# 512-query passes, row-tiled scores in a six-bank ring, and a convolution with half the weight loads

## The chip, the cores and the metric

The kernel runs on one core of one Trainium2 chip. The metric is the device time of one execution in microseconds (us). A ratio is always taken between kernels that ran on one chip in the same rounds. Engines are named as in the profile: PE is the matrix engine, PEld its weight loads, DVE VectorE, ACT ScalarE, POOL GpSimd, and SP the engine that issues most DMAs. "L594" is line 594 of that kernel.

## The reference

Two independent halves share the program. Half A is a long convolution, half B is attention with 32 heads of only 20 channels. Cut to what matters:

```python
S, D = 2048, 640                       # B = 1, bfloat16
def A(q, k, v, shift_k, ssm_k, ssm_D):
    kv = causal_fir4(k, shift_k) * v                   # 4 taps per channel
    y  = causal_conv(kv, ssm_k)                        # 2048 taps per channel (by FFT in the reference)
    return q * (y + kv * ssm_D)
def B(x, wqkv, wo):                                    # H = 32 heads, Dh = 20
    q, k, v = heads(x @ wqkv)
    p = softmax(q @ k.T * Dh**-0.5)                    # 32 x 2048 x 2048 exponentials
    return concat(p @ v) @ wo
out = concatenate([A, B], axis=-1)
```

The exponentials alone are 32 x 2048 x 2048 elements. On 128 partitions that is 1024 activations of 128x1024.

## The kernel before

Attention works in 1024 steps over (256 queries, group of four heads, 128 keys). A step computes scores for four heads at once with a block-diagonal Q (`QBD`), so that the 128-row array multiplies mostly zeros. It takes one exponential of 128x1024 and, every third step, the values of three steps. The convolution runs as filler between steps: it is a Toeplitz matrix product per quad of four channels, 64 matmuls with 64 weight loads, whose weights are overlapping windows of the taps. These "tap loads" read the same taps 32 times, each time shifted by one element.

```python
def hk_load(qi, waits=()):                       # tap loads of one channel quad
    for X, ch in enumerate(quad_channels(qi)):   # four channels, one DMA each
        src_ = _ap(kext_ap, [[1, 32], [1, HKW]], offset=ch * KXL)
        dst = HKring[32 * X:32 * X + 32, slot, :]
        ... sp.dma_start(dst, src_)
...
def S_group(n):                                  # scores of a step: two matmuls, 128 x 512
    lhsT = KT_all[:, g, kb * 128:(kb + 1) * 128]
    for qb in range(2):
        ins = pe.matmul(o, lhsT, QBD[:, g % 2, qb, :], start=True, stop=True)
...
# loop: EXP(n); S_group(n + 2); every third step PV_group x 3; then fillers with a budget of 620 ns
for dl in range(NTB):                            # 16 x 4 convolution matmuls per quad
    for q in range(4):
        lhsT = HKring[:, slot, col0:col0 + 128]
        ... pe.matmul(bank, lhsT, rhs, ...)      # 64 columns each
```

The softmax here doesn't subtract the row's maximum and nothing guards it: scores larger than these inputs give would overflow.

## Time and profile before

| | us |
|---|---|
| time, median of 3 runs | 1298.89 (1294.61 to 1301.39) |
| profiled span | 1304.2 |
| ACT busy, all exponentials | 1013 |
| PE busy | 1117 |
| first exponential starts | 80.7 |

From the page of the kernel before: busy time by engine, the granted PE clock and the DMA rate in 40 slices of 32.6 us, the chain of waits that ended last, and the groups of the exponentials and of the two largest PE jobs (line, operation, shapes, count; busy us and mean ns of one; idle before it and what ended that idle).

```profile
PE 1117.0 (86%) x17563; PEld 650.2 (50%) x17852; DVE 516.0 (40%) x1138; ACT 1014.5 (78%) x1025; POOL 23.6 (2%) x22
...
PEclk9998999799999998998999999999998998999997
...
GB/s 192 93 110 76 101 102 110 1 79 104 109 115 86 96 111 79 104 110 72 106 104 118 72 94 116 108 91 109 106 116 84 95 105 78 116 53 53 85 36 11
...
PE 68%; DVE 13%; ACT 12%; DMA 3%; issue 3%; SPq 1%; ACTq 0%; DVEq 0%
...
L635 ACT ACTIVATE P_sb<-PS 128x1024 bf16<-128x1024 f32 x1024 | 1013.2, 1024 | 273.3 <-PE PS L618 178.2
L618 PE MATMUL PS<-QBD,KT_all 128*128 128x512 bf16 x1759 | 559.1, 388 | 50.2 <-ACT P_sb L635 30.6
...
L556 PE MATMUL PS<-R,HKring 128*128 128x64 bf16 x10240 | 419.8, 193 | 0.0
```

PE and ACT are both nearly full (86% and 78%), and the chain lies mostly on PE. ACT has the work that cannot shrink. The timeline of the kernel before has one undisturbed run of exponentials near its end:

```profile
1224.46 64.11 ACT L635 ACTIVATE P_sb<-PS 128x1024 bf16<-128x1024 f32 x67
```

64.11 us for 67 exponentials is 0.957 us each, while one alone lasts 1.024 us: they overlap. By this figure ACT could do all 1024 in an estimated 980 us if it were never kept waiting. By stages (columns: stretch, its length, busy us and instructions per engine, granted PE clock, mean busy share of the 16 DMA engines, GB/s):

```profile
core 0: us, PE busy (x) PEld busy (x) DVE busy (x) ACT busy (x) POOL busy (x), PEclk, DMA share, GB/s
600.00:800.00 200.00, 186.89 (x3407) 117.30 (x3463) 70.21 (x152) 170.66 (x173) 0.00 (x0) 0.98 0.37 103
```

173 exponentials in 200 us, instead of the 209 that 0.957 us would allow.

### The profile page before, as it was taken

What the parts mean: (1) busy time and instruction counts of PE and PEld (TensorE: products, weight loads), DVE (VectorE), ACT (ScalarE), POOL (GpSimd) and SP (SyncE); (2) the same over time, 40 slices, a digit from 0 to 9 for tenths busy, and PEclk for the clock granted to TensorE, in tenths of its full rate; (3) what the DMA queues carried; (4) which work ended last, traced back from release to release, by engine and by line L of the source; (5) the groups of instructions that cost most, each with busy time, mean ns of one, the idle gap of its engine ahead of it and who ended that gap; (6) DMA issues with size and microseconds to landing.
All of it is one profiled execution on the core that took longest, in us unless ns stands there. A gap on an engine that the chain in (4) does not pass through costs nothing.

```text
span 1304.2 us, 38928 instructions
## 1 busy us (share of the span) xinstructions
PE 1117.0 (86%) x17563; PEld 650.2 (50%) x17852; DVE 516.0 (40%) x1138; ACT 1014.5 (78%) x1025; POOL 23.6 (2%) x22
## 2 busy tenths in 40 slices
PE   0487777699998998998999889999998998998776
PEld 0254432156665655655656456666665555663222
DVE  0376774533424423433442432443343343224521
ACT  0035568689997897986989779989997886989995
POOL 5100000000000000000000000000000000000000
PEclk9998999799999998998999999999998998999997
DMA  9632334023343342332334234333342332411210
GB/s 192 93 110 76 101 102 110 1 79 104 109 115 86 96 111 79 104 110 72 106 104 118 72 94 116 108 91 109 106 116 84 95 105 78 116 53 53 85 36 11
DMA packets 62260, 120.87 MB, mean 93 GB/s; under 512 B 23009, under 2 KB 40175, under 8 KB 62095
## 3 DMA queue, kind: packets, MB, share of 16 engines
q1 hardware_dynamic: 60974, 114.89, 32.5%
q0 software_dynamic: 1120, 3.48, 1.1%
q8 instruction: 140, 2.29, 0.7%
q14 instruction: 26, 0.20, 0.0%
HBM read 110.26 MB, written 8.03 MB: 91 GB/s over the span
## 4 chain that ended last, share of the span: by engine, by line
PE 68%; DVE 13%; ACT 12%; DMA 3%; issue 3%; SPq 1%; ACTq 0%; DVEq 0%
PE PS L618 25%; PE PS L556 23%; ACT P_sb L635 12%; PE PS L661 9%; PE PS L296 4%; DVE R L525 4%; DVE QBD L341 3%; PE PS L347 3%; DMA Dbc<-in_A_ssm_D_dram 2%; PE PS L769 2%; DVE R L418 2%; DVE R L416 2%; PE PS L682 1%; SPq L229 1%; DVE KT_all L329 1%
## 5 line engine op out<-in xcount | busy, mean ns | idle before, releaser
L635 ACT ACTIVATE P_sb<-PS 128x1024 bf16<-128x1024 f32 x1024 | 1013.2, 1024 | 273.3 <-PE PS L618 178.2
L618 PE MATMUL PS<-QBD,KT_all 128*128 128x512 bf16 x1759 | 559.1, 388 | 50.2 <-ACT P_sb L635 30.6
L556 PEld LDWEIGHTS PS<-R,HKring 128*128 128x128 bf16 x10240 | 373.7, 98 | 141.1 <-issue 50.7
L556 PE MATMUL PS<-R,HKring 128*128 128x64 bf16 x10240 | 419.8, 193 | 0.0
L570 DVE CAST R<-PS 128x64 bf16<-128x64 f32 x160 | 70.5, 440 | 353.3 <-PE PS L556 351.8
L618 PEld LDWEIGHTS PS<-QBD,KT_all 128*128 128x128 bf16 x2048 | 139.0, 98 | 102.4 <-ACT P_sb L635 92.3
L661 PE MATMUL PS<-P_sb,V_sb 128*21 128x256 bf16 x4096 | 184.5, 280 | 2.2 <-ACT P_sb L635 0.6
L661 PEld LDWEIGHTS PS<-P_sb,V_sb 128*21 128x21 bf16 x4096 | 75.4, 91 | 171.5 <-issue 137.8
L341 DVE CAST QBD<-PS 20x256 bf16<-20x256 f32 x256 | 107.6, 420 | 85.8 <-PE PS L347 79.6
L296 PE MATMUL PS<-xT,R 128*128 128x256 bf16 (+1 forms) x300 | 51.4, 310 | 73.0 <-DVE R L264 49.2
L525 DVE CAST R<-PS 32x512 bf16<-32x512 f32 x80 | 103.3, 1291 | 15.6 <-PE PS L514 13.7
L296 PEld LDWEIGHTS PS<-xT,R 128*128 128x128 bf16 x300 | 29.3, 106 | 97.0 <-DVE R L264 49.2
L674 DVE CAST OT_sb<-PS 128x256 bf16<-128x256 f32 x64 | 27.4, 428 | 126.9 <-PE PS L661 126.7
L347 PE MATMUL PS<-xT,Wq_pad 128*128 128x256 bf16 x315 | 47.2, 283 | 30.2 <-DVE R L525 30.2
L347 PEld LDWEIGHTS PS<-xT,Wq_pad 128*128 128x128 bf16 x315 | 30.8, 100 | 48.9 <-DVE R L525 34.2
L774 DVE CAST Bout<-PS 128x320 bf16<-128x320 f32 x32 | 15.7, 492 | 55.7 <-PE PS L769 41.4
L329 DVE CAST KT_all<-PS 128x256 bf16<-128x256 f32 (+1 forms) x60 | 25.4, 439 | 29.3 <-PE PS L296 29.0
L699 DVE RECIPROCAL rden<-PS 128x4 f32<-128x4 bf16 x128 | 23.4, 182 | 28.3 <-PE PS L682 26.1
L682 PE MATMUL PS<-ident,OT_sb 128*128 128x128 bf16 x128 | 19.0, 233 | 17.0 <-DVE QBD L341 10.9
L769 PE MATMUL PS<-Wo_sb,OnT_sb 128*128 128x320 bf16 x160 | 29.8, 321 | 3.6 <-DVE Bout L774 3.0
L706 DVE TENSOR_TENSOR O_norm<-PS,rden 128x80 bf16<-128x80 bf16 x128 | 30.9, 241 | 4.4
L682 PEld LDWEIGHTS PS<-ident,OT_sb 128*128 128x128 bf16 x128 | 8.3, 100 | 47.0 <-DVE QBD L341 38.7
(43 smaller groups left out, 225.1 us busy)
## 6 DMA issues: line engine op xcount, KB each, us to landing
HKring<-kext_scratch SPq DMA_DIRECT2D x640, 134.0 KB, 2.8
R<-in_A_k_dram SPq DMA_DIRECT2D x61, 160.0 KB, 2.6
R<-in_A_v_dram SPq DMA_DIRECT2D x16, 160.0 KB, 3.0
kext_scratch<-in_A_ssm_k_dram POOLq DMA_DIRECT2D x1, 2560.0 KB, 13.4
out_dram<-Bout SPq DMA_DIRECT2D x16, 160.0 KB, 1.8
qstage<-in_A_q_dram SPq DMA_DIRECT2D x16, 160.0 KB, 2.3
out_dram<-Aout SPq DMA_DIRECT2D x16, 160.0 KB, 1.8
R<-in_B_wqkv_dram SPq DMA_DIRECT2D x1, 2400.0 KB, 10.9
```

The costliest lines, as they stand in the source:

```text
L296: ins = pe.matmul(region[:, 0:ncols], lhsT, rhs, start=(idx == 0), stop=(idx == n - 1))
L329: return dv.tensor_copy(KT_all[:, g, c0:c0 + w], region[:, 0:w])
L341: return dv.tensor_copy(dst, srcap)
L347: ev = misc_group_multi(lambda pe: [pe.matmul(misc_ps[:, 0:256], l, r, start=(i == 0), stop=(i == NCC - 1)) for i, (l, r, _) in enumerate( ...
L525: return dv.tensor_copy(dst, src_)
L556: ins = pe.matmul(bank, lhsT, rhs, start=is_first, stop=is_last)
L570: ev = ev_op("dve", dve_p, lambda dv: dv.tensor_copy(dst, src_), [Wt(SEM_CONV, val)])
L618: ins = pe.matmul(o, lhsT, rhs, start=True, stop=True)
L635: ins = act.activation(P_sb[:, pb, :], S_ps[:, par * 1024:(par + 1) * 1024], ACT.Exp, scale=scale)
L661: ins = pe.matmul(o, lhsT, rhs, start=(kb == 0), stop=(kb == NKB - 1), tile_position=(0, 32 * i))
L682: ins = pe.transpose(misc_bf[:, qt * 128:(qt + 1) * 128], OT_sb[:, qt * 128:(qt + 1) * 128], ident[:, :])
L769: ins = pe.matmul(misc_ps[:, 0:320], OnT_sb[:, cc, qt * 128:(qt + 1) * 128], Wo_sb[:, cc, eh * 320:(eh + 1) * 320], start=(cc == 0), stop= ...
```

## The change

Its intent is to relieve PE, so that ACT alone sets the pace. 512-query passes give 512 steps of two exponentials each. Scores become four 20-row matmuls at four row positions of the array. Their results go round a ring of six PSUM banks. All Q and K are projected once, into two full tensors, and x is transposed on PE rather than by DMA. The convolution is rearranged to half the matmuls. The diff rewrites nearly all of the 1000 lines. Its core, with cuts marked:

```diff
-            def fn(pe):
-                ins = None
-                lhsT = KT_all[:, g, kb * 128:(kb + 1) * 128]
-                for qb in range(2):
-                    rhs = QBD[:, g % 2, qb, :]
-                    o = S_ps[:, (2 * par + qb) * 512:(2 * par + qb + 1) * 512]
-                    ins = pe.matmul(o, lhsT, rhs, start=True, stop=True)
+            def pe(e):
+                for u in range(4):
+                    bk = 2 * ((2 * b + u // 2) % 3) + u % 2
+                    ins = e.matmul(bank[bk], KT[32 * u:32 * u + DH, g, kb * 128:(kb + 1) * 128],
+                                   QT[32 * u:32 * u + DH, g, qc * 512:(qc + 1) * 512],
+                                   start=True, stop=True, tile_position=(32 * u, 0))
+                return ins
 ... cut ...
-            for X, ch in enumerate(quad_channels(qi)):
-                src_ = _ap(kext_ap, [[1, 32], [1, HKW]], offset=ch * KXL)
-                dst = HKring[32 * X:32 * X + 32, slot, :]
-                val = ev_op("sp", hk_p[slot], lambda sp, dst=dst, src_=src_: sp.dma_start(dst, src_),
-                            list(waits) if X == 0 else ())
+            P.dma("sp", HK[qd % NHK], ap(kext, [[80 * KXL, 4], [1, 32], [1, HKW]], (320 * B + m) * KXL + 1),
+                  d_hk[qd % NHK], reads=[b_kext], writes=[cv["HK"][qd % NHK]])
 ... cut ...
+                    for d in range(16):
+                        for r1 in range(2):
+                            n = (16 - d) * 4
+                            lhsT = HK[slot][:, 64 + 128 * d - 64 * r1:64 + 128 * d - 64 * r1 + 128]
+                            rhs = sub(KVX[i], [[64, 2], [1, n]], ql * 256 + r1 * 128)
+                            o = sub(bank[MISC], [[256, 2], [1, n]], u * 64 + d * 4)
 ... cut ...
+            if b >= 24 and b % 5 == 0 and kv_next[0] < NKB:
+                kv_task(kv_next[0])
```

The lines inside the loop over d and r1 are cut too. In the loop over steps, all projections that are not needed at once run as fillers through one bank (`MISC`), one or two per step, in the first 93 steps. The convolution follows from step 124 on.

## The prediction

> **What bounds the kernel now.** Profiled span 1304 us. ACT is busy 1014 us (78%), PE 1117 us (86%) (page, part 1). ACT's work is 1024 exponentials of 128x1024, 1.024 us each by the groups; but the timeline shows a run of 67 of them in 64.11 us (from 1224 us), so 0.957 us apart when none waits: a floor of 980 us. The rest is
> - a prologue: the first exponential starts at 80.7 us; the chain of waits shows 13 us of transposing-DMA issues, 31 us until the last input lands, then 20 us of V projection;
> - 80 to 200 us: 71 exponentials only (windows), as K projections and kv fill PE and DVE;
> - 200 to 1200 us: about 0.86 exponentials per us instead of 1.045, losing some 170 us. The chain is 68% PE; ACT idles 273 us, 178 us of it for scores (groups). PE per step: two 512-column score matmuls (0.22 us apart), values, and 17 convolution matmuls 28 to 29 ns apart;
> - 16 us of tail.
>
> **What the change does.** Same 1024 exponentials, in 512 steps of two.
> - Scores: block-diagonal 128-row matmuls become four 20-row, row-tiled matmuls in four banks. If concurrent, 0.25 to 0.3 us per step against 0.86 for the same output. The before trace shows concurrency only for column tiles (12 value matmuls of 256 columns take 0.32 us, a quarter of their serial time). [...]
> - Convolution: 10240 matmuls of 64 columns (about 297 us at 29 ns) become 5120 averaging 68 columns, estimated 188 us, plus 160 small combining matmuls and three DVE operations per four channel quads. The taps loaded stay 86 MB, now within some 300 steps: about 150 GB/s.
> - Cost: three array modes per step instead of two per three. [...] about 0.11 us from the last value matmul to the next convolution one. So 0.35 us per 1.91 us step.
> - A step with convolution: scores 0.27 + values 0.25 + convolution 1.03 + switches 0.35 = 1.9 us, level with ACT's 1.914 us.
> - No transposing DMA; scores start after a quarter of x and a narrow slice of W. But V, K, Q and x transposes, about 122 tasks through one PSUM bank, fall into the first 93 steps.
>
> **Sum (estimates from the durations above).** First exponential at 20 us; floor 980; first 93 steps lose 50 (two tasks per step wait for each other's evacuation; each of 16 kv blocks holds DVE 3.9 us and the bank with it); convolution steps lose 20; tail 15. Total 1085 us.
>
> Predicted **1085 us, range 1050 to 1140** (8 in 10). Chances: faster by over 2% 0.97, within 2% 0.02, slower 0.01.
>
> **What will show it.** Groups: ACT still 1024 x 1.02 us, its idle down from 273 to about 100 us. Chain: ACT above half. Timeline: four score matmuls starting within 0.1 us. First exponential at 15 to 28 us. Windows: 40 to 180 us below 0.9 exponentials per us; the last 150 us at 1.04. Convolution done by about four fifths of the steps, so no tail of it. DMA in the middle 140 to 190 GB/s.
>
> **What would make it wrong.** Row tiles that serialise: scores 0.9 us, 2.3 us per step or more, about 1200 us or above. Switches dearer than 0.11 us, or small-column convolution matmuls slower than 29 ns: each 0.1 us per step adds 20 to 25 us. Tap loads too slow for a five-slot ring. In the other direction, early tasks hidden better than thought: 1045 us.

No term of the sum goes with them: 20 + 980 + 50 + 20 + 15 = 1085 us. The 0.25 to 0.3 us for the scores were the estimate for the case that row tiles run together. The 0.35 us for switches are about three times the 0.11 us seen in the trace; that a further switch costs as much was not shown. The 188 us for the convolution were an estimate too; one from the kernel before (29 ns for 64 columns, taken for fewer columns as well, and 0.22 us per 512 columns above that) comes to about 184 us.

## More of the kernel before

Where medians of different rounds are set side by side, the kernel before, which ran in all of them, had medians of 1294 to 1302 us. The record marks every run used here as fast.

## The result, and the profile after

The changed kernel took 1479.84 us, median of 4 runs (1475.57 to 1481.97), against 1296.75 us for the kernel before on the same chip. The ratio is 1.141 (95% interval 1.137 to 1.146). Ratios are the mean time of one kernel's fast runs over that of the other's of the same rounds, so not quite the ratio of the medians. It is 14% slower, where 16% faster was forecast.

The page of the changed kernel, the same lines as before:

```profile
PE 1015.2 (69%) x11344; PEld 478.6 (32%) x11344; DVE 273.5 (18%) x570; ACT 970.8 (66%) x1027; POOL 123.9 (8%) x100
...
PEclk7569888885685666676666676566666767555555
...
GB/s 143 159 1 37 88 68 91 94 72 109 72 76 106 106 107 106 106 106 106 116 103 109 104 128 109 107 106 106 106 106 106 106 106 94 83 17 1 1 0 19
...
DMA 45%; PE 23%; ACT 19%; DVE 8%; SPq 3%; issue 1%; ACTq 0%; DVEq 0%
DMA R<-kext_scratch 42%; ACT P_sb L430 19%; PE PS L314 6%; PE PS L594 5%; PE PS L418 4%; PE PS L443 4%; SPq L144 3%; PE PS L514 2%; PE PS L333 2%; DVE R L364 1%; DVE R L362 1%; DVE KT L321 1%; DMA R<-kv_scratch 1%; DVE QT L321 1%; DMA R<-in_B_x_dram 1%
...
L430 ACT ACTIVATE P_sb<-PS 128x1024 bf16<-128x1024 f32 x1024 | 968.3, 1056 | 483.8 <-PE PS L418 474.3
L594 PE MATMUL PS<-R 128*128 128x128 bf16 (+15 forms) x5120 | 297.5, 221 | 215.3 <-DMA R<-kext_scratch 215.3
...
L418 PE MATMUL PS<-QT,KT 20*128 20x512 bf16 x2048 | 273.6, 524 | 109.2 <-ACT P_sb L430 104.6
```

PE has less to do, as intended: 1015 us of busy time, at a clock of 0.67 on average against 0.97. The convolution matmuls fell from 10240 to 5120. But ACT now idles 484 us before its exponentials instead of 273. The chain has moved to a DMA, the load from `kext_scratch`, which is the tap load. PE stands still 215 us in front of convolution matmuls for it. The GB/s row of slices has 106 in slice after slice. A rate that constant suggests a ceiling somewhere, and at a share of the DMA engines of only about 0.3:

```profile
600.00:800.00 200.00, 131.68 (x1701) 80.59 (x1699) 16.39 (x37) 111.05 (x116) 21.42 (x16) 0.66 0.31 107
```

One quad of channels in the middle, from the timeline (start, length, engine, line, operation, count, and idle before it; lines of weight loads and DMA issues left out):

```profile
702.36 1.45 PE L594 MATMUL PS<-R 128*128 128x128 bf16 x15 [2.12 <-DMA R<-kext_scratch]
703.74 0.61 PE L418 MATMUL PS<-QT,KT 20*128 20x512 bf16 x4
704.29 0.61 PE L443 MATMUL PS<-P_sb,V_sb 128*21 128x512 bf16 x4
704.41 1.94 ACT L430 ACTIVATE P_sb<-PS 128x1024 bf16<-128x1024 f32 x2 [2.89 <-PE PS L418]
704.83 0.78 PE L594 MATMUL PS<-R 128*128 128x72 bf16 x17
707.50 1.19 PE L594 MATMUL PS<-R 128*128 128x128 bf16 x11 [1.89 <-DMA R<-kext_scratch]
708.62 0.61 PE L418 MATMUL PS<-QT,KT 20*128 20x512 bf16 x4
```

A quad's 32 convolution matmuls begin at 702.36, the next quad's at 707.50 (17 + 15 matmuls between), 5.1 us later. PE waits 1.89 us for the load. ACT waits 2.89 us, because the next scores stand in PE's queue behind the waiting convolution. The four score matmuls, at a granted clock of 0.50 here (702 to 710 us), run together: 0.61 us for four. A convolution off the critical path has become the critical path, because the scores are issued behind it on PE and start only after it (708.62 after 707.50).

The load moves 4 x 32 rows of 4224 bytes, 540,672 bytes. At 106 GB/s that takes 5.1 us, the period seen. The trace's packet records show packets of 4224 bytes with a median duration of 164 ns; from 600 to 800 us exactly four of them are in flight for 87% of the time. 4224 bytes in 164 ns is 25.8 GB/s; four of them make 103 GB/s. The first dimension of the load, `[80 * KXL, 4]`, is four as well. That it decides over how many DMA engines a load is spread was the assumption at this point, not yet shown. The kernel before has 32 in that place; its packet records show 16 tap packets in flight at once for 13% of the time from 600 to 800 us, and none for 49%.

### The profile page after: what moved, and what is told of

Same layout as the page of the kernel before. It is cut to its first block, busy times and chain, and to the rows that moved or that the text cites. A ratio compares the mean times of both kernels' runs of the same rounds, so it can differ in the third digit from the quotient of the medians.

```text
span 1480.1 us, 24848 instructions
## 1 busy us (share of the span) xinstructions
PE 1015.2 (69%) x11344; PEld 478.6 (32%) x11344; DVE 273.5 (18%) x570; ACT 970.8 (66%) x1027; POOL 123.9 (8%) x100
## 4 chain that ended last, share of the span: by engine, by line
DMA 45%; PE 23%; ACT 19%; DVE 8%; SPq 3%; issue 1%; ACTq 0%; DVEq 0%
DMA R<-kext_scratch 42%; ACT P_sb L430 19%; PE PS L314 6%; PE PS L594 5%; PE PS L418 4%; PE PS L443 4%; SPq L144 3%; PE PS L514 2%; PE PS L333 2%; DVE R L364 1%; DVE R L362 1%; DVE KT L321 1%; DMA R<-kv_scratch 1%; DVE QT L321 1%; DMA R<-in_B_x_dram 1%
## 5 line engine op out<-in xcount | busy, mean ns | idle before, releaser
L430 ACT ACTIVATE P_sb<-PS 128x1024 bf16<-128x1024 f32 x1024 | 968.3, 1056 | 483.8 <-PE PS L418 474.3
L594 PE MATMUL PS<-R 128*128 128x128 bf16 (+15 forms) x5120 | 297.5, 221 | 215.3 <-DMA R<-kext_scratch 215.3
L594 PEld LDWEIGHTS PS<-R 128*128 128x128 bf16 x5120 | 262.9, 115 | 292.0 <-DMA R<-kext_scratch 223.6
L418 PE MATMUL PS<-QT,KT 20*128 20x512 bf16 x2048 | 273.6, 524 | 109.2 <-ACT P_sb L430 104.6
L443 PE MATMUL PS<-P_sb,V_sb 128*21 128x512 bf16 x2048 | 271.2, 521 | 3.7 <-DVE V_sb L338 2.5
L571 POOL COPY R<-R 32x512 bf16<-32x512 bf16 x80 | 107.2, 1339 | 724.8 <-PE PS L594 714.1
L418 PEld LDWEIGHTS PS<-QT,KT 20*128 20x128 bf16 x2048 | 54.4, 96 | 255.9 <-ACT P_sb L430 203.1
L314 PE MATMUL PS<-R 128*20 128x512 bf16 x1280 | 106.3, 475 | 44.0 <-DVE KT L321 10.9
L514 PE MATMUL PS<-Wo_sb,OnT 128*128 128x320 bf16 x160 | 39.0, 401 | 22.9 <-DVE OnT L503 18.3
L333 PE MATMUL PS<-R 128*128 128x240 bf16 (+1 forms) x240 | 35.8, 291 | 16.4 <-DVE V_sb L338 9.2
L333 PEld LDWEIGHTS PS<-R 128*128 128x128 bf16 x240 | 21.3, 109 | 31.8 <-DVE V_sb L338 13.5
```

The costliest lines, as they stand in the source:

```text
L314: ins = e.matmul(bank[bk][32 * i:32 * i + DH, :], W_sb[:, cc, off + i * DH:off + (i + 1) * DH], xT[:, cc, c * 512:(c + 1) * 512], start=(c ...
L333: ins = e.matmul(bank[bk][:, 0:w], xT[:, cc, kb * 128:(kb + 1) * 128], W_sb[:, cc, 2 * D + h0 * DH:2 * D + h0 * DH + w], start=(cc == 0), ...
L418: ins = e.matmul(bank[bk], KT[32 * u:32 * u + DH, g, kb * 128:(kb + 1) * 128], QT[32 * u:32 * u + DH, g, qc * 512:(qc + 1) * 512], start=T ...
L430: P.op("act", lambda e, pr=pr, s0=s0: e.activation(P_sb[:, pr % NPS, :], PS[:, s0 * 512:s0 * 512 + 1024], ACT.Exp, scale=scale), reads=[bk ...
L443: ins = e.matmul(bank[OBANK][32 * u:32 * u + DH + 1, :], V_sb[:, kb, 4 * g + u, :], P_sb[:, (2 * b + u // 2) % NPS, (u % 2) * 512:(u % 2) ...
L514: ins = e.matmul(bank[bk][:, 0:320], OnT[:, i, cc, :], Wo_sb[:, cc, hf * 320:(hf + 1) * 320], start=(cc == 0), stop=(cc == NCC - 1))
```

## The experiments

Three theories were held against each other. E: the tap loads are confined to 4 of 16 engines (four packets in flight; no trace names the engines). C: the low PE clock (0.67 on average) is the cause, and the waits on taps come along with it. L: the latency of a ring of five loads limits, not the engines.

### 1. Four loads per quad (e1_split_taps)

```diff
-            P.dma("sp", HK[qd % NHK], ap(kext, [[80 * KXL, 4], [1, 32], [1, HKW]], (320 * B + m) * KXL + 1),
-                  d_hk[qd % NHK], reads=[b_kext], writes=[cv["HK"][qd % NHK]])
+            P.dmas("sp", [(HK[qd % NHK][32 * X:32 * X + 32], ap(kext, [[1, 32], [1, HKW]], (320 * B + m + 80 * X) * KXL + 1))
+                          for X in range(4)], d_hk[qd % NHK], reads=[b_kext], writes=[cv["HK"][qd % NHK]])
```

> The changed kernel with one edit: each tap load (528 KB, outermost dimension 4) is issued as four loads of 32 rows each, as the kernel before did. Theory E (the load is confined to 4 of the 16 DMA engines: about 4 packets of 4224 bytes in flight at 164 ns each is 103 GB/s, and the profile shows a constant 106 GB/s; 528 KB then need about 5 us per channel quad): idle of PE on tap loads falls from 215 us to under 30 us, DMA in the middle exceeds 130 GB/s, and the time falls to 1150 to 1250 us, depending on whether the granted clock recovers. Rival C (the halved TensorE clock, 0.67 on average, sets the pace of the middle: 3.2 us per convolution step): the wait on taps shrinks but the step stays above 2.8 us and the time stays above 1400 us. Rival L (latency of a ring of five loads, not engines): little change, 1400 us or more, since four loads of a quarter each have the same ring.

Measured: 1138.0 us (1133.35 to 1145.25), ratio to the kernel before 0.879 (0.874 to 0.885). That is 12 us faster than the stated range. A change of 14% slower has become one of 12% faster, by one statement. PE's wait on tap loads fell from 215 us to 1.0 us:

```profile
L594 PE MATMUL PS<-R 128*128 128x128 bf16 (+15 forms) x5120 | 218.9, 196 | 1.3 <-DMA R<-kext_scratch 1.0
```

The same 200 us of the middle, and one ordinary step (PE lines alone), in the kernel with split loads:

```profile
600.00:800.00 200.00, 173.84 (x2862) 105.09 (x2859) 46.13 (x98) 188.99 (x207) 37.43 (x28) 0.94 0.75 192
```

```profile
450.02 0.39 PE L418 MATMUL PS<-QT,KT 20*128 20x512 bf16 x4
450.34 0.40 PE L443 MATMUL PS<-P_sb,V_sb 128*21 128x512 bf16 x4
450.67 1.15 PE L594 MATMUL PS<-R 128*128 128x48 bf16 x27
451.85 0.39 PE L418 MATMUL PS<-QT,KT 20*128 20x512 bf16 x4
```

192 GB/s instead of 107, at a DMA share of 0.75; 16 tap packets are now in flight for the largest part of the time (28%), where four were before. 207 exponentials in 200 us instead of 116. The granted clock of this stretch went from 0.66 to 0.94 without being touched. So the low clock came with the waits for taps and did not cause them: theory C falls. In this stretch PE's longest idle was 9.5 us in the changed kernel and is 0.8 us here. (A low clock was also seen without such idles: in the changed kernel, from 1265 to 1465 us, no idle of PE is longer than 1.17 us, PE is busy 63% of the stretch, and the granted clock was 0.52. It cost almost nothing there, ACT being the limit, busy 197 of 200 us.) A step is now 1.83 us from one group of scores to the next (451.85 - 450.02): scores 0.32, values 0.33, 27 convolution matmuls about 1.0, the rest a wait for ACT.

### 2. No tap traffic at all (e2_no_taps)

```diff
-                                if qd + NHK < 160:
-                                    hk_load(qd + NHK)
```

> Wrong result on purpose: only the first five tap loads are made and their buffers are used for all 160 quads, so the middle has no tap traffic at all. It bounds what the tap loads cost, whatever the reason. Theory E: about as fast as the split loads, 1130 to 1230 us; if it is more than 40 us faster than them, 16 engines are still not enough. Rival C: above 1400 us.

Measured: 1137.59 us (1131.19 to 1141.27), the same as the split loads to 0.4 us. As four loads per quad the tap loads cost nothing measurable; as one load per quad they cost 342 us (1479.84 - 1137.59). The profile confirms that the traffic is gone:

```profile
600.00:800.00 200.00, 173.59 (x2832) 103.31 (x2827) 48.09 (x102) 189.40 (x207) 37.42 (x28) 0.93 0.11 28
```

This kernel is wrong on purpose, and the comparison with the reference passed it nevertheless. So that comparison is too coarse to vouch for the taps; the split loads are as right as the changed kernel by their addresses, not by that check alone.

### 3. A ring of three (e3_ring_of_three)

```diff
-NHK = 5
+NHK = 3
```

> The changed kernel with three tap buffers instead of five. Theory E (rate of four engines): the rate of loads does not depend on the depth, so within 3% of the changed kernel's 1480 us, and the middle still moves about 100 GB/s. Rival L (latency): the rate scales with the depth, 3/5 of it, so the middle of 850 us grows to about 1400 us and the time to about 2000 us.

Measured: 1503.91 us (1495.11 to 1505.58), 1.6% above the changed kernel's 1479.84, and 108 GB/s between 600 and 800 us, with four tap packets in flight for 87% of the time as before:

```profile
600.00:800.00 200.00, 137.95 (x1743) 83.39 (x1741) 17.78 (x41) 115.65 (x122) 26.72 (x20) 0.63 0.30 108
```

Two fifths of the ring were taken away and the rate stayed. Theory L, which wanted about 2000 us, falls.

### 4. Two loads per quad, each with an outermost dimension of 2 (e8_two_loads_of_two)

```diff
-            P.dma("sp", HK[qd % NHK], ap(kext, [[80 * KXL, 4], [1, 32], [1, HKW]], (320 * B + m) * KXL + 1),
+            P.dmas("sp", [(HK[qd % NHK][64 * X:64 * X + 64],
+                           ap(kext, [[80 * KXL, 2], [1, 32], [1, HKW]], (320 * B + m + 160 * X) * KXL + 1)) for X in range(2)],
```

> The changed kernel with each tap load issued as two loads of 264 KB, each with an outermost dimension of 2 (the same rows, bytes and packets). Theory E [...]: two engines, so half the rate, about 53 GB/s in the middle, 10 us per channel quad, and about 2250 to 2350 us in all. Rival N (what helped in the split was more and smaller loads in flight, not their shape): faster than the changed kernel's 1480 us, somewhere between it and the 1138 us of four loads. If two such loads landed on different engines, the rate would stay at 106 GB/s and the time at 1480 us.

It was run on another chip. Measured: 2281.64 us (2 runs, 2279.7 and 2283.59), inside the stated range; ratio to the kernel before, on that chip, 1.752 (1.744 to 1.761).

```profile
600.00:800.00 200.00, 80.93 (x903) 48.60 (x903) 9.25 (x21) 59.74 (x62) 16.06 (x12) 0.52 0.13 53
```

53 GB/s at a DMA share of 0.13, which is 2/16. More and smaller loads made it worse, so it was not the number of loads that helped in experiment 1 but their shape. The packet records show exactly two tap packets in flight for 95% of the time: two loads of two did not bring four packets into flight. The trace does not name the engines: whether both loads shared the same two, or ran strictly one after the other, is not shown.

### 5. The opposite edit in the kernel before (b1_before_merged_taps)

```diff
-            for X, ch in enumerate(quad_channels(qi)):
-                src_ = _ap(kext_ap, [[1, 32], [1, HKW]], offset=ch * KXL)
-                dst = HKring[32 * X:32 * X + 32, slot, :]
-                ... one dma_start each ...
+            ch = quad_channels(qi)[0]
+            src_ = _ap(kext_ap, [[8 * KXL, 4], [1, 32], [1, HKW]], offset=ch * KXL)
+            dst = HKring[:, slot, :]
+            ... one dma_start ...
```

> The kernel before with the opposite edit: its four 134 KB tap loads per channel quad become one load of 536 KB with an outermost dimension of 4. Theory E: these loads run on 4 engines at about 103 to 106 GB/s, so a quad's taps take about 5.1 us, where the convolution of the kernel before consumes a quad every 5.7 us or so on average (160 quads from 230 to about 1150 us) and faster in undisturbed steps: 820 us of loads just fit into the 920 us, so the loss is partial, 1310 to 1420 us, with new waits of PE on tap loads of 20 us or more in the groups. If the outer dimension is harmless outside the changed kernel, 1290 to 1300 us and no such waits.

Measured: 1321.91 us (1314.63 to 1325.02) against 1294.04 us, ratio 1.021 (1.014 to 1.028; on the edge of the 2% at which a difference is called one). The time is in the range, but the waits of PE on tap loads did not come: none is listed. The packet records have four tap packets in flight for 80% of the time from 600 to 800 us, as expected; the kernel before consumes slowly enough that this just suffices. Its loss shows elsewhere. From the waits of the kernel before and of this one (who waited for whom: us in total, times, longest us):

```profile
DVE Bout L774 <- DMA out_dram<-Bout: 14.4, 7, 4.2
```

```profile
DVE Bout L773 <- DMA out_dram<-Bout: 29.8, 6, 8.3
PE PS L768 <- DVE Bout L773: 17.5, 7, 5.0
```

VectorE waits twice as long for the output stores, and PE behind it 17.5 us (3.0 us in the kernel before). Start for start, the exponentials of this run fall behind those of the kernel before in three steps of 5 to 7 us each (by 293, 447 and 611 us), just after VectorE's three waits of about 8 us for a store (at 282, 436 and 591 us), and hardly elsewhere. So the loss sits there; what held the stores up was not shown.

### 6. x before everything else (e4_x_first, e5_split_x_first)

The early part of the changed kernel also lost more than forecast. One wait stands out:

```profile
52.36 0.71 PE L293 MATMUL PS<-ident,R 128*128 128x128 bf16 x5 [17.70 <-DMA R<-in_B_x_dram]
```

The second half of x waits on the SP queue behind the first k and v loads, whose issue alone takes 29 us there.

```diff
-            P.dma("sp", Wo_sb, ...)        # moved, with the next three, from the setup
-            P.dma("sp", Dbc, ...)
-            kst_load(0)
-            kst_load(1)
 ...
+            if b == 12:                    # ... into step 12 of the loop
+                P.dma("sp", Wo_sb, ...)
+                P.dma("sp", Dbc, ...)
+                kst_load(0)
+                kst_load(1)
```

> The changed kernel with the loads of k, v, the output weights and D moved from the start into step 12 of the loop, so that the second half of x follows the first without waiting behind them on the queue. The profile of the changed kernel shows PE waiting 17.7 us at once for x at 34 to 52 us. If that wait is a loss that stays, the time falls by 12 to 25 us (1455 to 1468 us) and exponential number 20 comes at about 45 instead of 65 us. If it is given back later in the tap-bound middle, no change.

Measured for e4_x_first: 1459.43 us (1458.74 to 1466.47), 20 us less than the changed kernel; the wait for x fell from 17.7 to 5.0 us. Exponential 20 came at 53 us instead of 69, not at 45 as expected.

> Both earlier edits at once: split tap loads and x loaded before k, v and the output weights. If the early wait for x is a loss of its own, it adds to the gain of the split loads (1138 us): 1110 to 1125 us. If it is absorbed, 1133 to 1143 us.

Measured for e5_split_x_first, with the split loads as well: 1127.95 us (1124.53 to 1129.75), against 1138.0 us with split loads alone (another round on the same chip; the kernel before moved by 1.4 us between the two). The gain adds, but only 10 us of it, 3 us short of the stated range. In the profiled runs the stretch up to exponential 186 lost 12 us less than with split loads alone, and the convolution stretch after 248 lost 10 us more; why is open.

### 7. The kv blocks out of VectorE's way (e6_kv_after_projections, e7_kv_on_pool)

A kv block is the four-tap filter of half A for 128 positions: eight VectorE operations in a row. The changed kernel has one every fifth step. From the timeline of the kernel with split loads, around one of them (lines in between left out):

```profile
201.27 0.49 DVE L362 TENSOR_TENSOR R<-R 128x640 bf16<-128x640 bf16 x1
201.79 0.49 DVE L364 TENSOR_TENSOR R<-R 128x640 bf16<-128x640 bf16 x1
202.32 0.49 DVE L365 TENSOR_TENSOR R<-R 128x640 bf16<-128x640 bf16 x1
202.73 0.40 DVE L338 CAST V_sb<-PS 128x240 bf16<-128x240 f32 x1
203.19 2.31 PE L314 MATMUL PS<-R 128*20 128x512 bf16 x20 [2.33 <-DVE V_sb L338]
206.10 1.94 ACT L430 ACTIVATE P_sb<-PS 128x1024 bf16<-128x1024 f32 x2 [3.27 <-PE PS L418]
```

The cast of V at 202.73 had to wait for the block. It empties the one bank that all projections use, so PE waited 2.33 us for it. The projection that follows then took 2.31 us, where a like one at 212.57 took 1.25 us, and ACT starved 3.27 us. Theory K: the blocks cause most of the early loss. Rival P: the projections' own work causes it.

```diff
 # e6: later, and the convolution from step 151 on
-            if b >= 24 and b % 5 == 0 and kv_next[0] < NKB:
+            if b >= 93 and b % 3 == 0 and kv_next[0] < NKB:
 # e7: at the old steps, on the idle engine
-            P.op("dve", lambda e: e.tensor_tensor(tA, k[:, 0, :], Ctile[:, 0, :], ALU.mult),
+            P.op("pool", lambda e: e.tensor_tensor(tA, k[:, 0, :], Ctile[:, 0, :], ALU.mult),
 ... and the three other statements of kv_task likewise
```

Both are built on e5_split_x_first.

> The last one, with the 16 kv blocks (eight VectorE operations, about 4 us each) moved from steps 24 to 99, where they stand in front of the projections' evacuations on VectorE, to steps 93 to 138, after the last projection; the convolution starts at step 151 instead of 124. Theory K (each kv block holds up the evacuation of the one bank that all projections share, PE waits 2.3 us at a time and its clock halves): each block costs 3 to 4 us, the time falls by 40 to 65 us against the last one, to 1050 to 1080 us, and the clock between 120 and 330 us rises. Rival P (the projections' own PE work and their pairing in one bank cost the time): under 15 us.

Measured for e6_kv_after_projections: 1086.64 us (1077.97 to 1090.43), 41 us less than e5_split_x_first: the range of the gain is met at its edge, the time of 1050 to 1080 missed by 7 us. The early part did gain more: exponential 248 came at 307 us instead of 358. Some was given back in the later stretch, where its convolution now starts. The clock from 120 to 330 us, which was to rise, stayed at 0.81 on average: it was 0.99 against 0.85 up to 245 us, while projections ran, but 0.56 from 245 to 310 us, before the convolution filled PE again.

> Split taps and x first, with the kv blocks at their old steps but on GpSimd, which is idle then. Theory K: about as good as moving them, 1050 to 1085 us[...]. Rival P: within 15 us of the kernel with split taps and x first.

Measured for e7_kv_on_pool: 1068.24 us (1061.44 to 1075.21), ratio to the kernel before 0.826 (0.820 to 0.831). Two windows of 80 us, of e5_split_x_first and of e7_kv_on_pool:

```profile
120.00:200.00 80.00, 59.87 (x696) 19.38 (x688) 41.04 (x80) 51.89 (x55) 0.00 (x0) 0.85 0.23 73
```

```profile
120.00:200.00 80.00, 67.77 (x872) 24.80 (x864) 26.70 (x48) 73.18 (x79) 75.31 (x55) 0.98 0.32 102
```

55 exponentials became 79, and the clock 0.85 became 0.98. PE's waits of over 0.5 us in front of projections fell from 52 to 15 us, in this run and in e6_kv_after_projections. Rival P falls: it allowed 15 us, and 60 were gained. How the 60 us divide between waits and clock is not shown. An operation of a kv block took 1.40 us on GpSimd against 0.49 us on VectorE, 2.9 times as long; it was worth it still: the profile lists no wait of PE, ACT or VectorE for these operations. This is the fastest kernel: it takes 28% less time than the changed kernel and 17% less than the kernel before.

## Why the prediction was wrong

The forecast was a sum of terms. Here it stands against the runs, read off the traces by the start of the exponential of that number; a "loss" is the time of a stretch of the profiled run less 0.921 us per exponential. The last row is the median of the timed runs. The 0.921 us come from the chain of waits of the changed kernel (in order of time: start, us, what), which has pieces like this one near its end, 29 exponentials in 26.70 us:

```profile
1349.41 26.70 ACT P_sb L430 x29
```

| term | predicted | changed kernel | split taps | split, x first, kv on POOL |
|---|---|---|---|---|
| first exponential | 20 | 18 | 19 | 16 |
| floor, 1024 exponentials | 980 | 943 | 943 | 943 |
| loss to number 186 (the first 93 steps) | 50 | 126 | 120 | 56 |
| loss from 186 to 248 | 0 | 5 | 5 | 1 |
| loss from 248 to 838 (convolution) | 20 | 371 | 28 | 32 |
| tail after the last exponential starts | 15 | 16 | 16 | 16 |
| time | 1085 | 1480 | 1138 | 1068 |

- **The step that failed** is this sentence of the prediction: "The taps loaded stay 86 MB, now within some 300 steps: about 150 GB/s." It is a demand, and it was entered as if supply followed it. The same bytes in less time need a rate, and the rate of the new load was never worked out. The diff showed a first dimension of 4 where the kernel before had 32, and the prediction does not use it. With four packets in flight the rate was 106 GB/s, and the convolution stretch lost 371 us instead of 20. Experiments 1, 2, 3 and 4 show it: up to 16 tap packets in flight 1138 us, four 1480 us, two 2282 us, no traffic 1138 us, another depth the same rate (108 GB/s). "Tap loads too slow for a five-slot ring" was named as a risk, but without a size and outside the range.
- **Why the damage was so large.** The wait sits in front of a filler, but the scores issued behind it on PE wait as well, ACT starves, and the clock is low (0.66 from 600 to 800 us, against 0.94 with split loads): "A step with convolution" of 1.9 us held with split loads (1.83 us, in a stretch at a clock of 0.97); in the changed kernel it was 4.9 us from one group of scores to the next (703.74 to 708.62), with one wait for taps and a clock of 0.50.
- **Early loss, mis-sized.** "First 93 steps lose 50": it was 126. Moving kv off VectorE took 60 us from the time and x first took 10 to 20 us. The mechanism was in the prediction ("each of 16 kv blocks holds DVE 3.9 us and the bank with it"); not counted was that PE's clock fell with these waits (0.85 against 0.98 in the two windows above). What remained with kv on POOL, 56 us, is about what had been forecast for all of it.
- **The floor, mis-sized the other way.** 0.957 us per exponential is the mean of a run that was taken for undisturbed. Start for start, most of its exponentials follow 0.90 to 0.92 us apart, but about every third comes 1.04 to 1.12 us after the one before it. The changed kernel's runs have 0.90 to 0.92 us throughout, so 0.921 us each. Over 1024 that is 37 us less, which hid about half of the early error. So it is partly luck that, with supply put right, 1138 us would have lain just inside the range.
- **Right:** scores at four row positions do run together (four 512-column matmuls in 0.39 us with split loads, in a stretch at a clock of 0.97; in the kernel before one lasts 0.38 us and the next starts 0.22 us later, so four in a row would take an estimated 1.03 us, 2.6 times as long); the convolution matmuls at 37 ns on average (27 in about 1.0 us; the forecast, 188 us for 5120, says the same); a step no longer than forecast (1.83 us against 1.9), so the gaps between its three kinds of matmul no dearer in sum; the first exponential at 18 us; no convolution tail; the tail itself.
- **Marks of the prediction that failed:** ACT idle "down from 273 to about 100" (484); chain "ACT above half" (19%, DMA 45%); "DMA in the middle 140 to 190 GB/s" (107). With the loads split, the chain (61%) met its mark and DMA (192 GB/s) all but met it; ACT's idle, 155 us, was still half as much again.

Left open: the 28 to 47 us still lost in the convolution stretch of the kernels with split loads, the projections' share of the early loss, why ACT's spacing differs between the two rings, and the exact cause of the 28 us in experiment 5.

## What to carry to other kernels

When a change moves the same bytes in less time, work out the supply as well as the demand: read the outermost dimension of each DMA, with which the number of tap packets in flight changed here (four with 4, two with 2, up to 16 with 32), and see whether the needed rate fits. In this case's profiles, a DMA rate that is the same in every slice, at a mean share near k/16 (0.31 with k = 4, other loads included; 0.13 with k = 2), with one load in the chain, was a load with k packets in flight, and not the most that the memory gives: as four loads per quad the same taps moved at 192 GB/s. And a filler that can wait for a DMA is safe only while it does not wait: here it stopped the work behind it on PE, and PE's clock was 0.66 instead of 0.94.
